# Fused attention and MLP block: the last head group of the last 256 queries in two passes, w_mod in three loads, and new settings for the order planner

## Chip, cores, metric

One core of one Trainium2 chip. The metric is device time of the core in microseconds (us). Engines are named as the profile has them: PE (TensorE products, with PEld for its weight loads), ACT (ScalarE), DVE (VectorE), POOL, SP (issues the transfers).

## The reference

One transformer block on 2048 tokens of 640 channels, bf16, 32 heads of 20, MLP width 1536. Cut to what matters:

```python
mod = (silu(c) @ w_mod).reshape(1, 6, 1, -1)            # sa, ca, ga, sb, cb, gb
h = layernorm(x) * (1 + ca) + sa
x = x + ga * attention(h, wqkv, wo)                     # 32 heads, softmax over 2048 keys
h = layernorm(x) * (1 + cb) + sb
x = x + gb * mlp(h, w1, b1, w2, b2)                     # layernorm, gelu (tanh form), inside
```

## The kernel before

The program lists every operation with an estimated duration, and a greedy planner in Python simulates the five engines and fixes, before the kernel is built, the order of each engine's instructions. At run time each engine goes through its list in order. An estimate is therefore never a time, but it decides the order.

The work is cut into head groups (4 heads) and query chunks. A tile is 512 columns of scores for one head: PE makes them, ACT takes the exp of two tiles at once, PE multiplies with V. DVE takes some tiles off ACT with a three-instruction polynomial. "Fillers" are products with zeros that only keep PE's clock up. The last 512 queries are two halves, HA (queries 1536 to 1791) and HB (1792 to 2047); their head groups 5 to 7 come last, HA's and then HB's.

```python
dma("sp", wm0[:, :, 0:D], wmod_v[:, :, 0:D], 819200)          # byte count: for the planner only
dma("sp", wm0[:, :, D:2 * D], wmod_v[:, :, D:2 * D], 819200)
...
for m in range(10):                                          # shift (0-4), scale (5-9) of the first layer norm
    for kt in range(KD):
        mm(bb[:, m:m + 1], wm0[:, kt, m * 128:(m + 1) * 128], s_col[:, kt:kt + 1], ..., name="mod")
...
# HA's section: partial sums of wo over head groups 0-4, for HA and HB
for i in range(8):
    add(h0 + P0 + P1 * i, 0.9 * P1, lambda pace, i=i: wo_job(HA + i // 4, ..., range(GS), None, "part"))
run_chunk(seq, aux, ...)
# HB's section
seq = [(HB, g) for g in range(GS, NG)]
...                                                          # HA: rest of wo, layer norm, transposes
run_chunk(seq, aux, lambda s: s < HS, 1e9)                   # DVE may take exps up to mark HS = 16 of 32
# after the last exp: PV, row sums, rest of wo, layer norm of both HB tiles, then
for ft in range(NL, KF): m1_act(HA, ft, 4, [acts[-1]])       # NL = 0; gelu, so behind the last exp's table
...
for i in range(4): ...                                       # m2 of HA
tr2(ci, [None] * 3, ["dve", "act", "dve"], prio=3)           # transposes of HB, 256 columns
for ft in range(KF): m1_act(ci, ft, 4)                       # m1 of HB
for i in range(2 * nt): ...                                  # m2 of HB
```

m1 is the first MLP product with its gelu, m2 the second; wo is the attention's output product.

The softmax here doesn't subtract the row's maximum and nothing guards it: scores larger than these inputs give would overflow.

## Time and profile before

| | before |
|---|---|
| median of 3 runs | 866.95 us (866.79 to 867.98) |
| span of the profiled run | 865.8 us, mean clock 0.996 |
| exp tiles on ACT / on DVE | 1695 / 353 |
| first score product | 19.91 us |
| end of the last exp | 829.67 us |
| from there to the end | 36.1 us |
| fillers on PE, 750 to 830 us | 10.5 us |

How to read it: the span falls into a start (until exps run without a gap), a long middle in which ACT is never free, and a tail after the last exp, in which ACT no longer matters.

### The profile page before, as it was taken

The page shows a single profiled execution, that of the slowest core. Times are in us where ns is not written, and L with a number is a line of the kernel's source. Part 1 is how long each engine was busy: PE and PEld are TensorE (multiplying, and loading weights), DVE is VectorE, ACT ScalarE, POOL GpSimd, SP SyncE. Part 2 cuts the span into 40 slices and gives each one's busy share as a digit, 9 for nine tenths or more (in the row PEclk, how much of TensorE's full clock was granted, in tenths as well). Part 3 has the DMA queues.
Part 4 walks back from the last instruction along what each step waited for, and adds up shares of the span by engine and source line. Part 5 has one row for each costly group of instructions (what it writes and reads, how often), then busy time and mean ns, then how long its engine had stood idle before and what let it go on. Part 6 is the DMA issues. An engine that isn't in the chain of part 4 may idle for free.

```text
span 865.8 us, 16443 instructions
## 1 busy us (share of the span) xinstructions
PE 851.4 (98%) x6626; PEld 294.3 (34%) x6626; DVE 790.2 (91%) x1587; ACT 824.9 (95%) x892; POOL 195.0 (23%) x462
## 2 busy tenths in 40 slices
PE   8999999999999999999999999999999999999998
PEld 3433333333332222323233333233333322333365
DVE  6948899999999999999999999999999999999571
ACT  3999999999999999999999999999999999999962
POOL 5500100026010000399102550000019200010020
PEclk8999999999999999999999999999999999999999
DMA  9500000011010001600000100101000000000000
GB/s 293 160 2 4 23 13 14 14 32 70 15 42 4 14 14 34 205 14 14 14 1 21 37 29 15 44 1 44 29 15 14 14 14 13 11 27 16 16 8 31
DMA packets 29071, 30.14 MB, mean 35 GB/s; under 512 B 11202, under 2 KB 23362, under 8 KB 28994
## 3 DMA queue, kind: packets, MB, share of 16 engines
q1 hardware_dynamic: 28994, 29.08, 10.6%
q8 instruction: 52, 0.85, 0.4%
q14 instruction: 25, 0.20, 0.1%
HBM read 26.07 MB, written 2.88 MB: 33 GB/s over the span
## 4 chain that ended last, share of the span: by engine, by line
PE 46%; DVE 28%; ACT 22%; DMA 3%; issue 0%; POOL 0%; SPq 0%; DVEq 0%
ACT arena L1040 20%; PE psum L749 19%; PE psum L1023 17%; DVE arena L1050 8%; DVE arena L1056 8%; PE psum L1087 8%; DVE arena L1053 5%; PE psum L835 3%; DMA arena<-in_B_w_dram 2%; DVE arena L1379 2%; ACT arena L1386 1%; DVE arena L945 1%; DMA arena<-in_w_mod_dram 1%; PE psum L755 1%; DVE arena L950 1%; DVE arena L1095 1%
## 5 line engine op out<-in xcount | busy, mean ns | idle before, releaser
L1040 ACT ACTIVATE arena<-psum 128x1024 bf16<-128x1024 f32 x846 | 781.3, 1103 | 4.8 <-PE psum L1023 3.4
L1023 PE MATMUL psum<-arena 32*128 32x512 bf16 (+1 forms) x2240 | 362.6, 365 | 4.6 <-ACT arena L1040 1.6
L749 PE MATMUL psum<-arena 128*128 128x320 bf16 (+6 forms) x1704 | 343.6, 308 | 4.6 <-DMA arena<-in_w_mod_dram 2.3
L1050 DVE TENSOR_SCALAR arena<-psum 128x512 f16<-128x512 uint16 x353 | 234.1, 679 | 17.7 <-PE psum L1023 16.2
L1056 DVE SCALAR_TENSOR_TENSOR arena<-psum,arena 128x512 uint16<-128x512 f32 x353 | 236.4, 680 | 2.6
L1023 PEld LDWEIGHTS psum<-arena 32*128 32x128 bf16 x2240 | 94.3, 91 | 274.0 <-ACT arena L1040 206.0
L1087 PE MATMUL psum<-arena 128*32 128x512 bf16 (+1 forms) x2240 | 182.4, 368 | 0.7 <-DVE arena L1095 0.7
L749 PEld LDWEIGHTS psum<-arena 128*128 128x128 bf16 (+1 forms) x1704 | 126.0, 97 | 156.9 <-issue 104.0
L1133 POOL TENSOR_TENSOR arena<-arena 128x128 bf16<-128x128 bf16 x124 | 52.9, 455 | 529.2 <-DMA arena<-scr 529.2
L1053 DVE TENSOR_TENSOR arena<-arena 128x512 f16<-128x512 f16 x353 | 147.8, 437 | 1.6
L835 PE MATMUL psum<-arena 128*128 128x512 bf16 (+3 forms) x278 | 83.8, 376 | 0.0
L1087 PEld LDWEIGHTS psum<-arena 128*32 128x32 bf16 x2240 | 43.4, 92 | 90.6 <-issue 79.8
L1358 POOL TENSOR_TENSOR arena<-arena 128x128 bf16<-128x128 bf16 x120 | 51.1, 455 | 9.9 <-DVE arena L903 9.9
L1301 POOL TENSOR_TENSOR arena<-arena 128x128 bf16<-128x128 bf16 x105 | 44.1, 454 | 19.7 <-DVE arena L1216 18.4
L891 DVE BATCH_NORM_STATS2 arena<-arena 128x6 f32<-128x320 bf16 x96 | 43.5, 477 | 0.4
L835 PEld LDWEIGHTS psum<-arena 128*128 128x128 bf16 x278 | 23.5, 99 | 39.5 <-issue 33.2
L1399 DVE TENSOR_TENSOR arena<-psum,arena 128x320 bf16<-128x320 f32 x32 | 15.5, 484 | 21.9 <-PE psum L749 21.8
L950 DVE TENSOR_SCALAR arena<-psum,arena 128x512 bf16<-128x512 f32 x31 | 23.0, 741 | 6.9 <-PE psum L749 6.9
L898 POOL TENSOR_SCALAR arena<-arena 128x1 f32<-128x1 f32 (+1 forms) x40 | 9.5, 239 | 84.0 <-DVE arena L893 84.0
L1379 DVE TENSOR_SCALAR arena<-psum,arena 128x512 bf16<-128x512 f32 x36 | 26.6, 739 | 0.0
L1095 DVE CAST arena<-psum 128x512 bf16<-128x512 f32 (+1 forms) x35 | 22.2, 635 | 3.6 <-PE psum L1087 3.6
L899 POOL TENSOR_TENSOR arena<-arena 128x1 f32<-128x1 f32 (+1 forms) x40 | 24.9, 624 | 1.8
(56 smaller groups left out, 213.1 us busy)
## 6 DMA issues: line engine op xcount, KB each, us to landing
arena<-scr SPq DMA_DIRECT2D x29, 256.0 KB
arena<-in_A_x_dram SPq DMA_DIRECT2D x6, 640.0 KB, 5.3
arena<-in_B_w_dram SPq DMA_DIRECT2D x2, 1920.0 KB
arena<-in_w_mod_dram SPq DMA_DIRECT2D x2, 1600.0 KB
out_dram<-arena SPq DMA_DIRECT2D x16, 160.0 KB, 1.8
arena<-in_A_wqkv_dram SPq DMA_DIRECT2D x3, 800.0 KB
arena<-in_w_mod_dram SPq DMA_DIRECT2D x2, 800.0 KB
arena<-in_A_x_dram SPq DMA_DIRECT2D x4, 320.0 KB
```

The lines of the kernel that those rows point to most:

```text
L749: return P.op("pe", lambda e: e.matmul(outp, lhsT, rhs, start=start, stop=stop), R=[lhsT, rhs], W=[outp], dur=d, lat=d + 0.17, prio=prio, ...
L835: return lambda e: e.matmul(d_, zero, r_, start=new, stop=new, skip_group_check=True)
L1023: r = e.matmul(o_, lh, rh, start=True, stop=True, tile_position=(32 * hl, 0))
L1040: return e.activation(ring3[:, s_[0]:s_[1] + 1:s_[1] - s_[0], :], src, ACTF.Exp, scale=ESC, bias=EBIAS)
L1050: d1 = P.op("dve", lambda e: e.tensor_scalar(vw_, m_, -65536.0 * QRHO, math.sqrt(QK2) / 65536.0, op0=ALU.add, op1=ALU.mult), dur=t_, lat=t ...
L1053: d2 = P.op("dve", lambda e: e.tensor_tensor(vw_, vw_, vw_, op=ALU.mult), dur=t2, lat=t2 + 0.095, prio=DP, name="d2", lock=True)
L1056: x.emit = lambda e: e.scalar_tensor_tensor(out=o_, in0=pb, scalar=QS0, in1=vw_, op0=ALU.add, op1=ALU.add)
L1087: r = e.matmul(o_, lh, rh, start=(kt == 0), stop=(kt == TT - 1), tile_position=(0, 32 * hl))
L1133: pool(lambda e, d1_=d1_, r1_=r1_: e.tensor_tensor(d1_, d1_, r1_, op=ALU.mult), [d1_], [d1_, r1_], dur=0.1 + 0.0021 * PSTEP, prio=3, name= ...
L1301: pool(lambda e, t_=t_, s_=s_, r_=r_: e.tensor_tensor(t_, s_, r_, op=ALU.mult), [t_], [s_, r_], dur=0.1 + 0.0021 * (b - a), prio=7)
L1358: pool(lambda e, op=op, t_=t_, r_=r_: e.tensor_tensor(t_, t_, r_, op=op), [t_], [t_, r_], dur=0.1 + 0.0021 * (b - a))
L1379: dve(lambda e: e.tensor_scalar(d, bb, b_, None, op0=ALU.add), [bb, b_], [d], n, dur=0.1 + n / 900., prio=2, name="m1ev")
```

## The change

Three intents. In the tail: do the last head group of HB in two passes of 128 queries (HT0, HT1), so that tile 0's wo and layer norm run beside tile 1's exps and the MLP goes tile by tile; three of HA's twelve m1 jobs move into filler room before the last exp; HA's wo is done in one go, without partial sums, and HB's partial sums move from HA's section into HB's. At the start: w_mod in three loads with a second accumulator, and byte counts that make the planner see transfers land later. And settings of the planner: `QLAT` (a latency margin in us), `FAR` (look-ahead), `BACK` (limit of DVE's backlog), `FILL` (threshold for fillers). Cut to its core:

```diff
-NL = 0
-P0, P1, ... = 4, 2, 3, 1, 9, .7, 16, 0
-OKT, RB = 3, 550000
-QLAT, TIGHT, PAIR = 0.6, 8, 2
-NEAR, FAR, BACK = 9, 20, 2.2
-FLOOR, FILL, WARM = 3400, 5400, 3072
+WS = 1024
+NL = 3
+P0, P1, ... = 7.5, 0.5, 3, 1, 9, .7, 16, 0
+OKT, RB = 3, 300000
+QLAT, TIGHT, PAIR = .7, 8, 2
+NEAR, FAR, BACK = 9, 19, 2.0
+FLOOR, FILL, WARM = 3400, 5000, 3072
...
-        dma("sp", wm0[:, :, 0:D], wmod_v[:, :, 0:D], 819200)
-        dma("sp", wm0[:, :, D:2 * D], wmod_v[:, :, D:2 * D], 819200)
+        dma("sp", wm0[:, :, 0:D], wmod_v[:, :, 0:D], 1350000)
+        for a, b in ((D, WS), (WS, 2 * D)):
+            dma("sp", wm0[:, :, a:b], wmod_v[:, :, a:b], 1280 * (b - a))
...
-                    for tl in reversed(range(nt)):
+                    for tl in (range(nt) if mod and not after else reversed(range(nt))):
...
-            wo_job(ci, i // 2, i % 2, pace, range(GS, NG), "part", None, 0)
+            wo_job(ci, i // 2, i % 2, pace, range(NG), None, None, 0)
...
-        for i in range(8):
-            add(h0 + P0 + P1 * i, ...)                      # partial sums in HA's section
...
-        seq = [(HB, g) for g in range(GS, NG)]
+        seq = [(HB, g) for g in range(GS, NG - 1)] + [(HT0, NG - 1), (HT1, NG - 1)]
+        for i in range(4):                                  # HB's partial sums, in HB's section
+            add(P0 + P1 * i, 0.3, lambda pace, i=i: wo_job(HB, ..., range(GS), None, "part"))
...
+            if c == HT1:                                    # tile 0: row sums, wo, layer norm beside the exps
+                add(u + 0.5, 0.3, lambda pace: sel_job(HT0, NG - 1, pace, 1))
+                for half in range(2):
+                    add(u + U1 + U2 * half, ...wo_job(HB, 0, half, pace, range(GS, NG), "part", None, 0, 1))
+                add(u + U1 + 1.5 * U2, 0.3, lambda pace: ln2(HB, 0, True))
...
         for tl in range(nt):                                # MLP per tile of 128
+            tr2(ci, [None], [TE], prio=3, only=tl)
+            for ft in range(KF):
+                m1_act(ci, ft, 4 if tl else M0, [acts[-1]], tl)
             for half in range(2):
+                m2_late(ci, tl, half, 5 if tl else M2)
```

(One weight copy also goes from ACT to DVE at the start, the row sums get a buffer of their own, and more banks serve the first projections.)

More of the change, by code (lines that the diff above doesn't have):

```diff
@@ L14 @@
 DP = 3.5
-NL = 0
-P0, P1, HW0, HW1, HT, HM, HS, WP = 4, 2, 3, 1, 9, .7, 16, 0
+U1, U2, M0, M2, TE = 1.5, 0.5, 4, 5, "dve"
+WS = 1024
+NL = 3
+P0, P1, HW0, HW1, HT, HM, HS, WP = 7.5, 0.5, 3, 1, 9, .7, 16, 0
 VP = 3
-OKT, RB = 3, 550000
+OKT, RB = 3, 300000
 TRE, VE = (["act", "dve", "act"], ["dve", "dve", "dve"]), ("dve", "dve")
@@ L625, in bass_adaLN_cond__mha_block__mixer_channel_mlp__prompt_kernel @@
     QK2, QRHO, QS0 = 43.16024758, 0.50767267, -10.90298758
-    QS = [(0, 512), (512, 512), (1024, 512), (1536, 512), (1536, 256), (1792, 256)]
+    QS = [(0, 512), (512, 512), (1024, 512), (1536, 512), (1536, 256), (1792, 256), (1792, 128), (1920, 128)]
     LAST, HA, HB, GS = 3, 4, 5, 5
-    SLOT = (0, 1, 0, 1, 1, 1)
-    COL = (0, 0, 0, 0, 0, 256)
+    HT0, HT1 = 6, 7
+    SLOT = (0, 1, 0, 1, 1, 1, 1, 1)
+    COL = (0, 0, 0, 0, 0, 256, 256, 384)
     es = ExitStack()
@@ L718, in bass_adaLN_cond__mha_block__mixer_channel_mlp__prompt_kernel @@
         modc = V(alloc(64), [16], F32)
+        modc2 = V(alloc(64), [16], F32)
         b1col = V(alloc(64), [KF], F32)
@@ L794, in bass_adaLN_cond__mha_block__mixer_channel_mlp__prompt_kernel @@
         dma("sp", c_row[0:KD, :], c[0].rearrange("(kt p) -> kt p", p=128), 1280)
-        dma("sp", xb[0][:, 0:2, :], xsrc(0, 256), 327680)
-        dma("sp", xb[0][:, 2:4, :], xsrc(256, 256), 327680)
-        dma("sp", wm0[:, :, 0:D], wmod_v[:, :, 0:D], 819200)
-        dma("sp", wm0[:, :, D:2 * D], wmod_v[:, :, D:2 * D], 819200)
+        dma("sp", xb[0][:, 0:2, :], xsrc(0, 256), 560000)
+        dma("sp", xb[0][:, 2:4, :], xsrc(256, 256), 400000)
+        dma("sp", wm0[:, :, 0:D], wmod_v[:, :, 0:D], 1350000)
+        for a, b in ((D, WS), (WS, 2 * D)):
+            dma("sp", wm0[:, :, a:b], wmod_v[:, :, a:b], 1280 * (b - a))
         for w in (1, 0):
@@ L860, in bass_adaLN_cond__mha_block__mixer_channel_mlp__prompt_kernel @@
         dve(lambda e: e.tensor_copy(s_col, c_col), [c_col], [s_col], KD, prio=0)
-        bb = aux_bank()
+        bb, bb_ = aux_bank(), aux_bank()
+        WM = WS // 128
         for m in range(10):
             for kt in range(KD):
-                mm(bb[:, m:m + 1], wm0[:, kt, m * 128:(m + 1) * 128], s_col[:, kt:kt + 1],
+                mm((bb if m < WM else bb_)[:, m:m + 1], wm0[:, kt, m * 128:(m + 1) * 128], s_col[:, kt:kt + 1],
                    kt == 0, kt == KD - 1, 0, 1, cyc=130, name="mod")
         dve(lambda e, bb=bb: e.tensor_copy(modc[:, 0:5], bb[:, 0:5]), [bb[:, 0:5]], [modc[:, 0:5]], 5, prio=0)
-        dve(lambda e, bb=bb: e.tensor_scalar_add(modc[:, 5:10], bb[:, 5:10], 1.0), [bb[:, 5:10]], [modc[:, 5:10]],
-            5, prio=0)
+        for b_, m0, m1 in ((bb, 5, WM), (bb_, WM, 10)):
+            dve(lambda e, b_=b_, m0=m0, m1=m1: e.tensor_scalar_add((modc if m0 == 5 else modc2)[:, m0:m1], b_[:, m0:m1], 1.0), [b_[:, m0:m1]],
+                [(modc if m0 == 5 else modc2)[:, m0:m1]], 5, prio=0)
         for w in (1, 0):
@@ L876, in bass_adaLN_cond__mha_block__mixer_channel_mlp__prompt_kernel @@
                     pool(lambda e, dst=dst, src=src: e.tensor_copy(dst, src), [dst], [src], dur=0.5, prio=2)
+                elif w:
+                    act(dst, src, ACTF.Copy, n=400, prio=1)
                 else:
-                    act(dst, src, ACTF.Copy, n=400, prio=1)
+                    dve(lambda e, dst=dst, src=src: e.tensor_copy(dst, src), [src], [dst], 400, prio=2)
         for w in (1, 0):
@@ L907, in tr_jobs @@
         def tr_jobs(hn_tile, nt, dst, mod, prio, rels, engs, after=()):
-            for i, ktp in enumerate(((0, 1), (2, 3), (4,))):
+            for i, ktp in enumerate(((0, 1), (2, 3), (4,)) if nt > 1 else (tuple(range(KD)),)):
                 tb = aux_bank().bitcast(BF16)
                 for j, kt in enumerate(ktp):
-                    for tl in reversed(range(nt)):
+                    for tl in (range(nt) if mod and not after else reversed(range(nt))):
                         tr(tb[:, (j * nt + tl) * 128:(j * nt + tl + 1) * 128],
@@ L927, in tr_jobs @@
                     d = dst(kt, 1)
-                    s1, s2 = modc[:, 5 + kt:6 + kt], modc[:, kt:kt + 1]
+                    s1, s2 = (modc if 5 + kt < WM else modc2)[:, 5 + kt:6 + kt], modc[:, kt:kt + 1]
                     if engs[i] == "act":
@@ L1095, in pv_row @@
                 dve(lambda e: e.tensor_copy(d_, acc), [acc], [d_], n, prio=0, name="pvcopy")
+        rinv2 = V(o_kT + 3 * S * 2, [512], F32)
         def sel_job(ci, g, pace=NOPACE, prio=6, step=None):
@@ L1104, in sel_job @@
             for a in range(0, n, step):
-                s_, r_, d_ = bb[:, a:a + step], rinv[:, a:a + step], d[:, a:a + step]
+                s_, r_, d_ = bb[:, a:a + step], rinv2[:, COL[ci] + a:COL[ci] + a + step], d[:, a:a + step]
                 dve(lambda e, s_=s_, r_=r_: e.reciprocal(r_, s_), [s_], [r_], step, dur=0.07 + 3.2 * step / 512,
@@ L1162, in bass_adaLN_cond__mha_block__mixer_channel_mlp__prompt_kernel @@
                      dur=0.22, lat=0.4, prio=2, mode="f", name="warm", wc=512)
-                set_banks([5, 7])
+            set_banks([5, 7] if tc else [5, 7, 2, 3])
             for g in range(2):
@@ L1167, in bass_adaLN_cond__mha_block__mixer_channel_mlp__prompt_kernel @@
                     proj_job(g, 0, tc, g)
+            set_banks([5, 7])
             for tl in range(4):
@@ L1334, in wo_evac, with wo_job @@
             dve(lambda e: e.tensor_tensor(d, bb, s_, op=ALU.add), [bb, s_], [d], 320, prio=prio, name="x2")
-        def wo_job(ci, tl, half, pace, gs=range(NG), src=None, dst=None, prio=2):
+        def wo_job(ci, tl, half, pace, gs=range(NG), src=None, dst=None, prio=2, pp=6):
             bb = aux_bank()[:, 0:320]
-            mmjob(bb, wo_pairs(ci, tl, half, gs), 320, 6, pace, "wo")
+            mmjob(bb, wo_pairs(ci, tl, half, gs), 320, pp, pace, "wo")
             wo_evac(ci, tl, half, bb, prio, src, dst)
@@ L1362, in ln2, with tr2 @@
             normalize(hd, hd, tt, p, so=4)
-        def tr2(ci, rels, engs, prio=6):
+        def tr2(ci, rels, engs, prio=6, only=None):
             h2T = views(ci)[2]
+            if only is not None:
+                tr_jobs(lambda tl: hn_of(ci, only), 1, lambda kt, n: h2T[:, kt:kt + n, only * 128:(only + 1) * 128], False,
+                        prio, rels, engs)
+                return
             tr_jobs(lambda tl: hn_of(ci, tl), QS[ci][1] // 128, lambda kt, n: h2T[:, kt:kt + n, :], False,
@@ L1456, in bass_adaLN_cond__mha_block__mixer_channel_mlp__prompt_kernel @@
             add(h0 - 8, 0.1, lambda pace, x=x: load_x2(x))
-        for i in range(8):
-            add(h0 + P0 + P1 * i, 0.9 * P1, lambda pace, i=i: wo_job(HA + i // 4, i % 4 // 2, i % 2, pace, range(GS), None, "part"))
         run_chunk(seq, aux, lambda s: s >= TWO, TWO, (7, 4))
         aux.clear()
-        seq = [(HB, g) for g in range(GS, NG)]
+        seq = [(HB, g) for g in range(GS, NG - 1)] + [(HT0, NG - 1), (HT1, NG - 1)]
         add(0.5, 0.3, lambda pace: sel_job(HA, NG - 1, pace, 1, step=128))
@@ L1465, in bass_adaLN_cond__mha_block__mixer_channel_mlp__prompt_kernel @@
             add(HW0 + HW1 * i, 0.6, wo_late(HA, i))
+        for i in range(4):
+            add(P0 + P1 * i, 0.3, lambda pace, i=i: wo_job(HB, i // 2, i % 2, pace, range(GS), None, "part"))
         add(HT, 0.3, lambda pace: tr2(HA, pace.rels(3), ["dve"] * 3))
@@ L1470, in bass_adaLN_cond__mha_block__mixer_channel_mlp__prompt_kernel @@
         for j, (c, g) in enumerate(seq):
-            if j:
+            if c == HT1:
+                add(u + 0.5, 0.3, lambda pace: sel_job(HT0, NG - 1, pace, 1))
+                for half in range(2):
+                    add(u + U1 + U2 * half, 0.3, lambda pace, half=half: wo_job(HB, 0, half, pace, range(GS, NG), "part", None, 0, 1))
+                add(u + U1 + 1.5 * U2, 0.3, lambda pace: ln2(HB, 0, True))
+            elif c == HT0:
+                add(u + 0.5, 0.3, lambda pace: sel_job(HB, NG - 2, pace, 1, step=128))
+            elif j:
                 add(u + 2, 0.3, lambda pace, x=seq[j - 1]: sum_job(*x))
@@ L1482, in bass_adaLN_cond__mha_block__mixer_channel_mlp__prompt_kernel @@
             gelu(HA, NOPACE, after=[acts[-1]], loads=1.4, k=NL)
-        early = [(tl, half) for tl in range(nt) for half in range(2)]
+        early = [(1, half) for half in range(2)]
         wbank = {}
@@ L1489, in bass_adaLN_cond__mha_block__mixer_channel_mlp__prompt_kernel, with m1_act @@
         set_banks([7, 4, 5, 6])
-        sel_job(ci, NG - 1, prio=1, step=128)
-        def m1_act(ci, ft, prio, after=()):
-            n = QS[ci][1]
+        sel_job(HT1, NG - 1, prio=1)
+        def m1_act(ci, ft, prio, after=(), tl=None):
+            c0, n = (0, QS[ci][1]) if tl is None else (tl * 128, 128)
             bb = aux_bank()[:, 0:n]
             for i, (l, r) in enumerate(m1_pairs(ci, ft)):
-                mm(bb, l, r, i == 0, i == KD - 1, prio, n, name="m1")
+                mm(bb, l, r[:, c0:c0 + n], i == 0, i == KD - 1, prio, n, name="m1", rel=len(marks) - 1)
@@ L1497, in m1_act, with m2_late @@
             b_ = b1col[:, ft:ft + 1]
-            d_ = g1_of(ci)[:, ft, :]
+            d_ = g1_of(ci)[:, ft, c0:c0 + n]
             P.op("act", lambda e: e.activation(d_, bb, ACTF.Gelu_apprx_tanh, bias=b_), R=[bb, b_], W=[d_],
                  dur=n / 1200.0 + 0.235, lat=n / 1200.0 + 0.435, prio=2, name="gelu1", after=after)
+        def m2_late(ci, tl, half, prio=5):
+            bb = aux_bank()[:, 0:320]
+            for ft, (l, r) in enumerate(m2_pairs(ci, tl, half)):
+                mm(bb, l, r, ft == 0, ft == KF, prio, 320, name="m2")
+            finish_y(ci, tl, half, bb)
@@ L1502, in bass_adaLN_cond__mha_block__mixer_channel_mlp__prompt_kernel @@
         for ft in range(NL, KF):
             m1_act(HA, ft, 4, [acts[-1]])
+        for tl, half in early:
+            bb = wbank[(tl, half)]
+            (l, r), = wo_pairs(ci, tl, half, [NG - 1])
+            mm(bb, l, r, False, True, 3, 320, name="wo")
+            wo_evac(ci, tl, half, bb, 0, "part")
+        ln2(ci, 1, tail=True)
+        for i in range(4):
+            m2_late(HA, i // 2, i % 2)
+        set_banks(range(8))
         for tl in range(nt):
+            tr2(ci, [None], [TE], prio=3, only=tl)
+            for ft in range(KF):
+                m1_act(ci, ft, 4 if tl else M0, [acts[-1]], tl)
@@ L1505, in bass_adaLN_cond__mha_block__mixer_channel_mlp__prompt_kernel @@
             for half in range(2):
-                bb = wbank[(tl, half)]
-                (l, r), = wo_pairs(ci, tl, half, [NG - 1])
-                mm(bb, l, r, False, True, 3, 320, name="wo")
-                wo_evac(ci, tl, half, bb, 0, "part")
-            ln2(ci, tl, tail=True)
-        for i in range(4):
-            bb = aux_bank()[:, 0:320]
-            for ft, (l, r) in enumerate(m2_pairs(HA, i // 2, i % 2)):
-                mm(bb, l, r, ft == 0, ft == KF, 5, 320, name="m2")
-            finish_y(HA, i // 2, i % 2, bb)
@@ L1516, in bass_adaLN_cond__mha_block__mixer_channel_mlp__prompt_kernel @@
-        set_banks(range(8))
-        tr2(ci, [None] * 3, ["dve", "act", "dve"], prio=3)
-        for ft in range(KF):
-            m1_act(ci, ft, 4)
-        for i in range(2 * nt):
-            bb = aux_bank()[:, 0:320]
-            for ft, (l, r) in enumerate(m2_pairs(ci, i // 2, i % 2)):
-                mm(bb, l, r, ft == 0, ft == KF, 5, 320, name="m2")
-            finish_y(ci, i // 2, i % 2, bb)
+                m2_late(ci, tl, half, 5 if tl else M2)
         P.final = outs
```

## The prediction

> **What bounds the kernel now.** I read the busy table first, then the page in 40 slices, then narrow stretches at both ends, then the time-ordered chain and the time-ordered instructions of the tail.
>
> ```profile
> PE 851.4 (98%) x6626; PEld 294.3 (34%) x6626; DVE 790.2 (91%) x1587; ACT 824.9 (95%) x892; POOL 195.0 (23%) x462
> ACT  3999999999999999999999999999999999999962
> PEclk8999999999999999999999999999999999999999
> ...
> L1040 ACT ACTIVATE arena<-psum 128x1024 bf16<-128x1024 f32 x846 | 781.3, 1103 | 4.8 <-PE psum L1023 3.4
> L835 PE MATMUL psum<-arena 128*128 128x512 bf16 (+3 forms) x278 | 83.8, 376 | 0.0
> ```
>
> PE shows 98%, but 83.8 us of it are fillers (L835, they only keep the clock up). The engine without slack is ACT: its exps (L1040) fill all slices but the first and the last two. 781.3 us / 846 = 0.92 us for a pair of score tiles, 0.46 us for one 512-column tile. So three things decide the time: when the exps start, how many tiles DVE takes off ACT, and what is left after the last exp. The busy table by stretch (columns: length, then PE, PEld, DVE, ACT, POOL, granted clock, DMA share, GB/s):
>
> ```profile
> 12.00:18.00 6.00, 6.00 (x45) 3.67 (x43) 3.89 (x12) 3.49 (x6) 2.87 (x6) 0.50 1.00 337
> 24.00:30.00 6.00, 6.00 (x54) 2.56 (x52) 6.00 (x16) 6.00 (x8) 5.54 (x12) 1.00 0.20 44
> 791.00:808.00 17.00, 16.99 (x213) 6.66 (x208) 14.75 (x31) 17.00 (x20) 0.00 (x0) 1.00 0.02 2
> 808.00:820.00 12.00, 11.97 (x138) 4.50 (x136) 4.81 (x12) 12.00 (x15) 1.60 (x4) 1.00 0.08 26
> 832.30:847.30 15.00, 15.00 (x117) 11.01 (x118) 12.00 (x31) 5.68 (x12) 3.50 (x8) 1.00 0.04 13
> 848.50:863.00 14.50, 14.49 (x112) 10.54 (x112) 1.47 (x3) 5.71 (x13) 0.00 (x0) 1.00 0.07 24
> ```
>
> At the start PE runs at a clock of 0.50 while it is 100% busy. At the end PE is busy 29.5 of 29.5 us while ACT is at 38% and DVE idles in the second half. The chain of work that ended last says the same at both ends (start, length, what):
>
> ```profile
> 11.58 0.83 PE psum L749 x25
> 12.41 2.16 PE psum L755 x20
> ...
> 15.84 3.07 PE psum L749 x9
> 18.93 0.75 DVE arena L945
> ...
> 832.29 15.07 PE psum L749 x116
> ...
> 848.46 14.54 PE psum L749 x112
> 863.00 0.02 issue
> 863.02 0.49 DVE arena L1399
> ```
>
> **What the Trainium skill says.**
> 1. "TensorE: Matmul & The Clock Gate", Part 1: the array falls to half clock after an idle window of about 3.4 us and comes back after a busy one[...]. The trace agrees: PE idles from 7.6 to 9.4 and most of 11.0 to 11.6 (0.63, 0.00, 0.57 busy in the single microseconds 7 to 10), the products with w_mod are one column wide, and the clock is 0.50 from 11.4 to 17.9.
> 2. Same page, "Back-to-back issue gap": a sustained stream of weight load and 128-column product is put at about 81 ns. The trace disagrees: ten 128-wide transposes with a weight load each issue in 0.56 us, 56 ns apiece, and 25 one-column products with new weights take 0.76 us, 30 ns apiece. I use 56 ns.
> 3. "ScalarE: Activation LUTs", "What ACT_TABLE_LOAD costs": a table load is 1283 ns (the trace has 1.28 us before the gelu), and an activation with a pointer bias takes 280 ns + 0.833 ns per column, neighbours overlapping by 93 ns. For 128 columns that makes an estimate of 0.29 us; no such shape is in the trace.
>
> **The change part by part.**
>
> *Start.* The three loads of w_mod move the same bytes. The byte counts given to the scheduler become larger, so that its simulated landing is later; it should then put transposes and fillers where PE now waits (7.6 to 9.4, 11.0 to 11.6). Transposes go in tile order and the first three scale columns have their own accumulator, so evacuations can begin before the last w_mod part lands (11.57 now). One 0.53 us weight copy moves from ACT, where it sat between two evacuations of hT (14.06), to DVE. On the chain, PE work from 11.58 to 18.93 is 7.3 us, of which 6.5 at half clock. At full clock: mod products done at 12.35, 20 transposes 1.1 us (now 2.16) to 13.5, with the first evacuation at about 12.9; three ACT evacuations of 0.72 end at about 15.0; last K product and five Q products (0.22 each) to 16.3; Q evacuation 0.75; first scores at 17.1 where they are now at 19.9. **Start: -2.8 us.** It carries to the end, since ACT has no idle time from 23.1 on, as long as DVE (100% from 20 to 30) still prepares the next 512 tokens in time; that work moves forward too.
>
> *Exps.* 2048 tiles remain; a pass of 128 queries packs four key tiles in a 512-column tile, so ACT's work is the same. The 32 tiles of the last group need 8 score products of 128 columns where 4 of 256 stood: by 56 ns against 107 ns nothing to speak of, and 25 fillers (4.5 us) stood in the last 10 us of exps, so PE has room. But DVE gets other work. A tile on DVE costs about 1.46 us net of overlap (in 700 to 720: 20 us less 4.6 of other work, 10.5 tiles). Only the first 48 of the last 96 tiles may go to DVE; it now does 8 there (791 to 808), with some 3.5 us of other work and 2.25 idle. The old kernel's wo and second layer norm of the first 128-query tiles ran late (812 to 827), because a backlog of partial wo products on PE came first. The new one drops that partial sum for HA (8 products in one go), so these land on time, in the very stretch where DVE should take exps. Each layer norm is 4.1 us of DVE (2 x 0.49 + 0.21 stats twice, 0.40 norm twice, 2 x 0.50): I put about 5 us more there, 3 to 4 tiles fewer on DVE, 3.5 x 0.46 = 1.6 us more on ACT. Against it, three evacuations of 0.48 leave the stretch before (one tile more on DVE, -0.46). In the last 48 tiles DVE had 12 of 21.7 us to do; the new sum (sel of the sixth group 2.3, of the first pass 1.2, two wo 1.0, layer norm 4.1, three m1 evacuations 1.3) is about 10, and fits. The small knobs (look-ahead, DVE backlog, filler threshold) I take as nothing. **End of the exps: +1.0 us.**
>
> *Tail.* After the last exp (829.7) PE is the bound: 33.3 us to the last product. Leaving it, into PE's filler room before: 15 of 60 m1 products of HA (6.45 us / 60 = 107 ns each) 1.6 us; HA's ten transposes, 0.7; half of the early and final wo products, 4 x 0.156 + 2 x 0.14 = 0.9. Together 3.2. Coming in: m1 of the last 256 queries as 120 products of 56 instead of 60 of 107, +0.3; one small wait at the second tile's transposes, +0.1. The m2 sums (13 products, 1.975 each, eight of them) stay. **Tail: -2.8 us.**
>
> Sum: -2.8 + 1.0 - 2.8 = -4.6, on 866.95: 862.3 us.
>
> **Rivals.**
> - *The tail's chain through the last tile becomes the bound.* For tile 1: PV and its copy 1.7 us, row sums and reciprocal 1.9, wo 1.3, layer norm with POOL hops 6.4, transposes 1.2, m1 with twelve gelus 4, m2 4.0, all after 829.7: 20.5 us. PE has 30 us to do, and 20 us of it (nine m1, HA's m2, tile 0's MLP) need nothing from tile 1. So it should hide; if the order put m2 of HA too early or too late, PE would stand for 1 to 3 us: 864 to 865.
> - *The half tile is issue-bound.* At 81 ns for 128 columns the 120 products take 9.7 us, not 6.7: 3 us, and the tail gains nothing: 865.
> - *The start is held by transfers.* DMA is saturated from 3 to 24 us (share 1.0). w_mod's last part can't land before 11.57, and x comes after it. If the early clock is won but ACT then waits for hT of the second 512 tokens, the start keeps only 1 us: 864. For it: DVE is full from 20 to 30. Against it: ACT has 32 tiles, 14.7 us of work, from the first tokens.
> - *The knobs were retuned well.* If DVE takes 5 more tiles over the 700 us in the middle, that is another -2.3: 860. The trace (DVE 97% busy there) leaves little.
>
> **Range and chances.** The three terms have errors of about 1.5, 1.5 and 1.5 us, and the knobs 1: some 2.8 together, so 8 in 10 lie within about 3.6 on either side; I widen it a little on the fast side, since a change with so many settings was most likely tuned. 857.8 to 866.0. Two per cent is 17 us, more than half of the whole tail, and no path to it exists: within 2% 0.97, faster 0.02, slower 0.01.
>
> **What would show it.** Granted clock at 1.0 between 12 and 18 us and the first score product near 17 (start right; at 0.5 it is wrong). ACT dense from about 20.5. The last exp near 828 (829.7 - 2.8 + 1.0). DVE exps among the last 96 tiles down from 8 to about 5. From the last exp to the end 33.3 us where it is 36.1, PE without a gap over 0.5 us, 128-column m1 products at 56 ns. PE gaps in the tail, products at 80 ns, or an ACT gap between 25 and 40 us would each prove one term wrong.

## More of the kernel before

The stretches around the last exp, in the table of busy time by stretch (columns: length, then PE, PEld, DVE, ACT, POOL, clock, DMA share, GB/s):

```profile
790.00:829.67 39.67, 39.56 (x469) 15.63 (x469) 27.39 (x62) 39.66 (x44) 5.27 (x12) 1.00 0.04 12
829.67:832.29 2.62, 2.04 (x26) 1.19 (x25) 1.34 (x5) 1.28 (x1) 0.00 (x0) 1.00 0.03 6
832.29:863.00 30.71, 30.25 (x238) 22.15 (x238) 14.50 (x37) 11.96 (x25) 3.50 (x8) 1.00 0.05 17
```

PE is full before and behind the last exp, and only before it does it hold fillers.

## The result, and the profile after

861.57 us (859.86 to 862.16, 4 runs) against 867.19 in the same rounds: ratio 0.9931, 95% interval 0.9914 to 0.9948. A ratio is the mean time of one kernel's fast runs over that of the other's of the same rounds, so not quite the ratio of the medians. At a bar of 2% that counts as the same, to which the prediction gave 0.97. The predicted time was 862.3 in a range of 857.8 to 866.0. The total is right. The terms are not: this table compares the two profiled runs.

| | before | after | predicted for after |
|---|---|---|---|
| mean clock | 0.996 | 0.998 | (no cold window) |
| first score product | 19.91 | 20.26 | 17.1 |
| end of the last exp | 829.67 | 827.44 | 827.9 (-2.8 + 1.0) |
| exp tiles on DVE | 353 | 356 | fewer in the last 96, otherwise the same |
| last exp to the end | 36.1 | 33.0 | 33.3 |
| span | 865.8 | 860.4 | 861.2 |

The page of the changed kernel, lines as shown of before:

```profile
PE 836.7 (97%) x6710; PEld 296.0 (34%) x6768; DVE 797.5 (93%) x1601; ACT 821.5 (95%) x898; POOL 194.7 (23%) x460
L1049 ACT ACTIVATE arena<-psum 128x1024 bf16<-128x1024 f32 x845 | 779.4, 1105 | 4.4 <-PE psum L1032 3.8
L840 PE MATMUL psum<-arena 128*128 128x512 bf16 (+3 forms) x230 | 74.1, 394 | 0.0
```

Fillers fell by 9.7 us (83.8 to 74.1). Of the exp work on ACT, 2.7 us went (with the single tiles: 781.3 + 2.2 to 779.4 + 1.4), which is more than the 2.2 us by which the last exp came earlier. So the start gave nothing in this run. By 60 us its ACT had 37.9 us of exps done, that of the kernel before 38.8: it was even 0.9 us behind (one_pass, nl0 and hs24 below, with the same start and the same mean clock, had 38.5 to 38.8, so part of this is the single run). Its stretches say why:

```profile
9.00:10.00 1.00, 0.28 (x4) 0.11 (x3) 0.04 (x1) 0.00 (x0) 1.00 (x3) 1.00 1.09 321
11.00:12.00 1.00, 0.39 (x16) 0.30 (x13) 0.97 (x2) 0.00 (x0) 0.46 (x1) 1.00 0.67 171
12.00:13.00 1.00, 0.58 (x21) 0.44 (x19) 0.61 (x3) 0.00 (x0) 0.76 (x2) 1.00 0.79 168
13.00:14.00 1.00, 1.00 (x21) 0.88 (x19) 0.26 (x2) 0.59 (x2) 0.58 (x3) 0.97 0.92 326
16.00:17.00 1.00, 1.00 (x4) 0.38 (x3) 1.00 (x4) 0.00 (x0) 0.00 (x0) 0.50 1.04 371
```

PE still waits for w_mod and the clock is halved again, in one window (13.9 to 17.4) and no longer in two (11.1 to 18.0; the prediction reads 11.4 to 17.9). The last part of w_mod lands at 12.7, not at 11.6; DMA is only 0.67 to 0.79 busy while it comes. The tail, in the same table by stretch:

```profile
790.00:827.44 37.44, 37.34 (x571) 17.71 (x569) 29.85 (x69) 37.44 (x41) 4.22 (x12) 1.00 0.03 7
827.44:829.64 2.20, 1.28 (x25) 0.65 (x23) 0.65 (x2) 1.81 (x3) 0.45 (x1) 1.00 0.03 7
829.64:857.60 27.96, 27.76 (x275) 20.60 (x275) 12.71 (x31) 10.99 (x33) 2.42 (x6) 1.00 0.06 19
```

PE's part behind the table load fell from 30.71 to 27.96 us, without gaps. In the stretch before it PE idles 0.92 of 2.20 us; that wait is new and was not foreseen. The chain of waits names it (start, length, what):

```profile
826.39 1.36 PE psum L753 x9
...
827.81 1.28 ACT L1522
829.10 0.01 issue
829.11 0.48 ACT arena L1522
829.59 0.05 issue
829.64 0.24 PE psum L753
```

HA's m1 products are ready early, fill the four banks open to them, and PE then waits until ACT has loaded its gelu table (1.28 us) and emptied one. The same chain then runs through DVE, from 829.90 to 835.49 (last row sums, both layer norms), and PE waits 0.16 us for it at 835.5: up to there PE and DVE are all but tied. Fillers between 750 and 830 us fell from 10.5 to 3.3 us: the room that the moved work went into is nearly used up.

### The profile page after: what moved, and what is told of

The parts are those of the page before. It is cut to its first block, busy times and chain, and to the rows that moved or that the text cites. A ratio compares the mean times of both kernels' runs of the same rounds, so it can differ in the third digit from the quotient of the medians.

```text
span 860.4 us, 16684 instructions
## 1 busy us (share of the span) xinstructions
PE 836.7 (97%) x6710; PEld 296.0 (34%) x6768; DVE 797.5 (93%) x1601; ACT 821.5 (95%) x898; POOL 194.7 (23%) x460
## 4 chain that ended last, share of the span: by engine, by line
PE 48%; ACT 37%; DVE 12%; DMA 1%; issue 1%; SPq 0%; ACTq 0%
ACT arena L1049 35%; PE psum L753 18%; PE psum L1032 18%; PE psum L1096 9%; DVE arena L1059 3%; DVE arena L1065 3%; PE psum L840 3%; DVE arena L1062 2%; ACT arena L1402 1%; DMA arena<-in_w_mod_dram 1%; PE psum L759 1%; DVE arena L900 1%; DVE arena L959 1%; DVE arena L977 1%; DVE arena L1395 0%
## 5 line engine op out<-in xcount | busy, mean ns | idle before, releaser
L1049 ACT ACTIVATE arena<-psum 128x1024 bf16<-128x1024 f32 x845 | 779.4, 1105 | 4.4 <-PE psum L1032 3.8
L1032 PE MATMUL psum<-arena 32*128 32x512 bf16 (+2 forms) x2304 | 367.6, 359 | 9.3 <-DVE arena L1065 2.7
L753 PE MATMUL psum<-arena 128*128 128x320 bf16 (+6 forms) x1708 | 328.3, 300 | 8.3 <-issue 3.9
L1059 DVE TENSOR_SCALAR arena<-psum 128x512 f16<-128x512 uint16 x356 | 236.2, 680 | 14.4 <-PE psum L1032 12.7
L1032 PEld LDWEIGHTS psum<-arena 32*128 32x128 bf16 x2304 | 98.7, 91 | 266.8 <-ACT arena L1049 188.0
L1096 PE MATMUL psum<-arena 128*32 128x512 bf16 (+5 forms) x2304 | 181.7, 362 | 1.2 <-DVE arena L1104 0.7
L1096 PEld LDWEIGHTS psum<-arena 128*32 128x32 bf16 (+1 forms) x2304 | 44.3, 93 | 90.4 <-issue 78.7
L840 PE MATMUL psum<-arena 128*128 128x512 bf16 (+3 forms) x230 | 74.1, 394 | 0.0
L1395 DVE TENSOR_SCALAR arena<-psum,arena 128x512 bf16<-128x512 f32 (+1 forms) x39 | 28.1, 720 | 0.1
L959 DVE TENSOR_SCALAR arena<-psum,arena 128x512 bf16<-128x512 f32 x31 | 23.0, 742 | 4.7 <-PE psum L753 4.7
L912 DVE TENSOR_SCALAR arena<-arena 128x640 bf16<-128x640 bf16 x48 | 23.2, 497 | 3.0 <-POOL arena L908 3.0
L1104 DVE CAST arena<-psum 128x512 bf16<-128x512 f32 (+2 forms) x36 | 22.3, 621 | 3.3 <-PE psum L1096 3.3
```

The costliest lines, as they stand in the source:

```text
L753: return P.op("pe", lambda e: e.matmul(outp, lhsT, rhs, start=start, stop=stop), R=[lhsT, rhs], W=[outp], dur=d, lat=d + 0.17, prio=prio, ...
L840: return lambda e: e.matmul(d_, zero, r_, start=new, stop=new, skip_group_check=True)
L1032: r = e.matmul(o_, lh, rh, start=True, stop=True, tile_position=(32 * hl, 0))
L1049: return e.activation(ring3[:, s_[0]:s_[1] + 1:s_[1] - s_[0], :], src, ACTF.Exp, scale=ESC, bias=EBIAS)
L1059: d1 = P.op("dve", lambda e: e.tensor_scalar(vw_, m_, -65536.0 * QRHO, math.sqrt(QK2) / 65536.0, op0=ALU.add, op1=ALU.mult), dur=t_, lat=t ...
L1096: r = e.matmul(o_, lh, rh, start=(kt == 0), stop=(kt == TT - 1), tile_position=(0, 32 * hl))
```

## The experiments

Each kernel was timed in 5 rounds (null_dp in 6) beside the kernel before, but not beside the changed kernel; the median of the kernel before was 866.89 to 867.19 in the four sets of rounds. Instruction lists were compared too: in some variants they differ only around the edited place, in others the planner reorders thousands of lines in the middle. That decides what a variant can tell. Because runs differ in the cold window at the start, the means at a mean clock of 0.998 and of 1.0 stand beside the median. The changed kernel has only three runs at 0.998 (861.05 to 862.16) and one at 1.0, so a difference of less than about 1 us to it isn't clear of noise. "Exp end" and "tail" are of the profiled run.

| kernel | lists differ | median | ratio to before (95%) | mean at 0.998 / 1.0 | exp end | tail |
|---|---|---|---|---|---|---|
| changed kernel | | 861.57 | 0.9931 (0.9914 to 0.9948) | 861.77 / 859.86 | 827.44 | 33.0 |
| start_only | from before: start | 866.62 | 0.9990 (0.9976 to 1.0004) | 866.87 / 865.53 | 828.57 | 36.1 |
| start_undone | widely | 863.82 | 0.9962 (0.9950 to 0.9975) | 864.14 / none | 827.25 | 35.2 |
| one_pass | last section | 862.80 | 0.9955 (0.9943 to 0.9968) | 862.72 / none | 826.77 | 34.2 |
| old_knobs | widely | 863.91 | 0.9966 (0.9953 to 0.9978) | 863.74 / none | 829.31 | 33.1 |
| warm_start | start | 862.12 | 0.9943 (0.9931 to 0.9954) | 862.89 / 861.32 | 828.20 | 32.9 |
| two_loads | start | 860.49 | 0.9926 (0.9914 to 0.9939) | 861.63 / 860.13 | 826.77 | 32.9 |
| null_qlat | widely | 862.97 | 0.9953 (0.9941 to 0.9965) | 863.47 / 861.91 | 829.63 | 32.1 |
| null_dp | widely | 868.75 | 1.0016 (1.0004 to 1.0029) | 869.02 / 867.32 | 829.89 | 34.9 |
| warm_fill | from two_loads: 8 products | 861.27 | 0.9934 (0.9922 to 0.9947) | none / 861.29 | 826.64 | 33.0 |
| nl0 | tail | 862.66 | 0.9947 (0.9934 to 0.9959) | 862.53 / 860.85 | 827.08 | 33.8 |
| old_partials | last sections | 864.42 | 0.9975 (0.9961 to 0.9988) | 865.56 / 863.99 | 825.12 | 37.0 |
| hs24 | last section | 863.58 | 0.9959 (0.9947 to 0.9972) | 863.75 / 862.36 | 824.72 | 37.0 |

One run of null_dp (899.36 us at a clock of 0.96) is left out of its ratio. "Exp end" contains the luck of the start: the profiled runs of start_only, null_dp, warm_fill and old_partials had a clock of 1.0, that of start_undone 0.996, all others 0.998. All outputs were correct.

**start_only: the kernel before with the change's start.**

```diff
+        dma("sp", wm0[:, :, 0:D], wmod_v[:, :, 0:D], 1350000)
+        for a, b in ((D, WS), (WS, 2 * D)): dma(...)        # and the other edits of the start
```

> The kernel before with the change's start alone (three loads of w_mod, larger byte counts for the scheduler, transposes in tile order, second scale tile, one weight copy moved to DVE). Theory from the two traces: the start gained nothing, since in the changed kernel the first score product came at 20.26 us against 19.91 and the clock was still halved from 14.0 to 17.2: 866 to 868.5 us, same as before, unless a run escapes the cold window (then about 865.5). Rival, the prediction on record: the start is worth 2.8 us: about 864.4.

The ratio 0.999 is 0.9 us of gain, with an interval of 2.1 gained to 0.3 lost: a gain of 2.8 is out. The profiled run had a clock of 1.0, its first score product was at 18.28, and by 60 us ACT had 40.6 us of exps done where the kernel before had 38.8. So a warm start can win 1.9 us by then, but the last exp ended only 1.1 us earlier, and three of the five runs were not fully warm. At a mean clock of 0.998 its two runs (866.87) equal the three of the kernel before in the same rounds (866.90), so what the start gains it gains in warm runs.

**start_undone: the changed kernel with the old start.**

```diff
-        dma("sp", wm0[:, :, 0:D], wmod_v[:, :, 0:D], 1350000)
+        dma("sp", wm0[:, :, 0:D], wmod_v[:, :, 0:D], 819200)   # and the other edits of the start
```

> The changed kernel with the start of the kernel before. Theory: the start is worth nothing, so all of the gain stays: 861 to 862.5 us. Rival (prediction on record): the start carries half of the gain, so 864.4 us.

It lost 2.3 us in the median, near the rival's number, but not where the rival says: its last exp ended at 827.25, no later than with the new start. Its tail is 2.2 us longer. The planner had reordered the whole list, and in that order most of HA's early m1 work slid behind the last exp (PE has 59 products of 256 columns there, the changed kernel 46). So this run doesn't measure the start; start_only does.

**two_loads and warm_start: what in the start matters.**

```diff
 two_loads
-        for a, b in ((D, WS), (WS, 2 * D)):
+        for a, b in ((D, 2 * D),):
 warm_start
-        dma("sp", wm0[:, :, 0:D], wmod_v[:, :, 0:D], 1350000)
+        dma("sp", wm0[:, :, 0:D], wmod_v[:, :, 0:D], 1700000)
-                   ..., cyc=130, name="mod")
+                   ..., cyc=70, name="mod")
```

> The changed kernel with w_mod in two loads as before; the two scale tiles and all else stay. Order of instructions differs only near the start. Theory: the third load gives nothing: its last part landed at 12.7 us (11.6 before) with DMA only 0.67 to 0.79 busy[...]; with two loads the last part lands about 0.5 us earlier and the time is the same or 0.5 us less: 861.0 to 861.6. Rival: the earlier first evacuations are what the third load buys, and without it the start loses 1 us: 862.6.

> The changed kernel, with the scheduler told that the first part of w_mod lands 1 us later and that a one-column product takes 32 ns (70 columns) and not 57, so that it puts fillers into the waits between the three parts of w_mod. Instruction order differs from the changed kernel's only in the first 50 us. Theory: the clock still halves in the changed kernel because PE is only 0.28 to 0.68 busy from 9 to 13 us; filled, the clock stays at 1.0 and ACT's exps start 1.5 to 2.5 us earlier: 859.5 to 860.5. Rival: the start is held by the last w_mod landing and by DVE (full from 20 to 30 us), so a warm clock is worth less than 0.7 us: 861 to 861.6.

With two loads the time is the same at either clock (861.63 against 861.77 at 0.998, 860.13 against 859.86 at 1.0). The third load buys nothing measurable. warm_start went against my theory: three of five runs were warm, yet it is no faster, since at a clock of 0.998 it is 1.1 us slower (862.89).

**warm_fill: two loads, and zero products where PE waits for w_mod.** It differs from two_loads by eight products and nothing else.

```diff
+  before the mod products of m = 0, 5, 8: 4, 3 and 1 of
+      e.matmul(psum[:, 3072:3584], zero, idr, start=False, stop=False, skip_group_check=True)
```

> The kernel with two loads of w_mod, all orders unchanged, with eight zero products of 512 columns put in where PE waits for w_mod (4, 3 and 1 of them). In the changed kernel and its variants, runs at a mean clock of 1.0 (no cold window at the start) are 1.5 to 1.9 us faster than runs at 0.998. Theory: with the waits filled every run has a clock of 1.0 and the median is that of the two-load kernel's warm runs, 860.1 (859.8 to 860.4), with no run above 861. Rival: the fillers push w_mod's products back or the window is cold anyway: 860.5 to 861.5, some runs at 0.998.

All five runs had a clock of 1.0, as the theory said, and lay within 0.6 us (861.05 to 861.63). From 9.60 to 13.01 us, the 3.41 us before the clock fell in two_loads, PE was busy 3.39 us here and 2.57 there. Five warm runs of five beside three of five is little by itself; but in the kernels with the changed kernel's own start (changed kernel, nl0, one_pass, old_partials, hs24) 6 of 24 runs were warm. That idle PE brings on the cold window is thus likely, not proven. The rival was right on the time: it is 1.2 us slower than the warm runs of two_loads. In the two profiles the last products with w_mod start at 13.16 where two_loads had them done by about 13.0; the first score product is at 18.72 against 19.78 with a cold clock, and ACT had 39.5 against 38.4 us of exps done by 60 us. But the last exp ended at 826.64 against 826.77: nearly all of that lead was gone by then.

**one_pass: the last group in one pass of 256, the old MLP order behind it; the rest of the change stays.**

```diff
-        seq = [(HB, g) for g in range(GS, NG - 1)] + [(HT0, NG - 1), (HT1, NG - 1)]
+        seq = [(HB, g) for g in range(GS, NG)]              # and the tail of the kernel before
```

> The changed kernel with the last head group of the last 256 queries in one pass of 256 and the old tail after it; the three early m1 products, the moved partial sums, the start and the knobs are kept. Theory: the split lets tile 0's wo, layer norm and row sums run beside the last exps, so it is worth about 1 us of PE (wo and sel) and removes the wait for tile 0's layer norm: 862.5 to 863.5. Rival: the tail's gain of 3.5 us is the split's nearly alone: about 865. Second rival: the split costs as much in 128-column products as it saves: 861.5.

Its tail is 34.2 us, 1.2 longer, and at a clock of 0.998 it is 0.95 us slower (862.72 against 861.77). The split itself is worth about 1 us of the tail's 3.2. As totals the intervals of the two ratios overlap, so the size rests on the trace and on equal clocks, and of the changed kernel's three runs at 0.998 one (862.16) comes within 0.3 us of one_pass's fastest (862.43).

**nl0 and old_partials: the work moved ahead of the last exp.**

```diff
 nl0
-NL = 3
+NL = 0
 old_partials
+        for i in range(8): add(h0 + 4 + 2 * i, ...)         # HA and HB partials in HA's section, as before
-        for i in range(4): add(P0 + P1 * i, ...)            # HB partials in HB's section
-            wo_job(ci, i // 2, i % 2, pace, range(NG), None, None, 0)
+            wo_job(ci, i // 2, i % 2, pace, range(GS, NG), "part", None, 0)
```

> The changed kernel with none of HA's m1 jobs before the last exp (NL 0 instead of 3). Only the last 50 us of the lists differ. Prediction on record: 15 products leave the tail, 1.6 us: 863.2. Rival: with NL 0 the products come back at 107 ns each, but the 0.9 us gap of PE at the table load (it waits for a free bank) and three DVE evacuations go, so the loss is only 0.5 to 1 us: 862.1 to 862.6.

> The changed kernel with the partial wo sums of both halves (HA, HB) back in HA's section, as before. Theory: the backlog on PE returns, HA's second layer norm comes after the 48th tile, HA's transposes and the three m1 jobs slip past the last exp, while DVE may do one or two exps more before it: 862.5 to 864. Rival (prediction on record taken alone): DVE then has about 5 us less before the 48th tile and the exps end 1 us earlier, and the time is the same or better: 860.5 to 861.6.

nl0: tail 33.8 (+0.8), 862.53 against 861.77 at 0.998 (+0.8). Fifteen products of 107 ns are 1.6 us. The rival's number came, its reason did not: the wait for a bank is there with `NL` = 0 too, 0.86 us at 829.27.

```profile
829.27 6.58 PE L753 MATMUL psum<-arena 128*128 128x256 bf16 x57 [0.86 <-ACT arena L1522]
```

Behind the last exp nl0 has 58 products of 256 columns, the changed kernel 46: 12 more and not 15, since three got ahead of it anyway. PE is busy 1.1 us longer there (30.17 against 29.04) and stands 0.2 us less.

old_partials is the most telling of all: it ran 3.8 us longer at a clock of 0.998 (865.56 in two runs, against 861.77), with a tail of 37.0 us. Its exps ended at 825.12, 2.3 us before the changed kernel's, but that is the start: its profiled run was warm, and by 60 us ACT was 2.5 us ahead. The table by stretch, exps on ACT alone, the changed kernel first:

```profile
0.00:60.00 60.00, 37.87 (x41) 0.97 0.53 164
0.00:60.00 60.00, 40.38 (x44) 1.00 0.53 164
```

ACT's instructions around the last exp, in order of time (start, length, what, idle before):

```profile
825.14 1.28 ACT L1522 ACT_TABLE_LOAD   x1
829.93 0.47 ACT L1522 ACTIVATE arena<-psum,arena 128x256 bf16<-128x256 f32 x1 [3.51 <-PE psum L753]
840.24 0.83 ACT L1402 ACTIVATE arena<-arena 128x768 bf16<-128x768 bf16 x1
```

ACT waits 3.5 us for HA's first m1 product, and the gelu of the three early m1 jobs comes at 840.24; in the changed kernel the first gelu follows the table load at once and that of the three jobs is at 832.24. HA's layer norm had come too late: DVE stands from 802.9 to 808.7 waiting for PE, which has an m2 and the last two partial sums still to do (evacuated at 808.66, 810.64 and 813.23), and HA's transposes, done before 820 in the changed kernel, start at 827.26. Behind the last exp PE runs 3.0 us of fillers, where the changed kernel has none. (DVE took no more exps than in the changed kernel: 356, and 5 where that took 6 in 790 to 808.)

**hs24: DVE may take exps of the first 72 of the last 96 tiles.**

```diff
-P0, P1, ... HM, HS, WP = 7.5, 0.5, ... .7, 16, 0
+P0, P1, ... HM, HS, WP = 7.5, 0.5, ... .7, 24, 0
```

> The changed kernel with DVE allowed to take exps in the first 72 of the last 96 tiles, not 48. Theory: DVE is only 5 to 8 of 10 us busy from 800 to 828 while ACT is full, so it takes 3 to 5 tiles more, worth 0.46 us each: 859.5 to 860.5. Rival: the exps on DVE hold up tile 0's wo evacuations and layer norm, which then slip into the tail: 861.5 to 863.

DVE did take 3 more tiles and the exps ended 2.7 us earlier, at 824.72 (0.9 us of that it was ahead by 60 us, at the same mean clock). The tail grew by 4.0 us and the kernel is 2.0 us slower at a clock of 0.998. The rival was right:

```profile
824.75 1.28 ACT L1522 ACT_TABLE_LOAD   x1
834.28 0.84 ACT L1402 ACTIVATE arena<-arena 128x768 bf16<-128x768 bf16 x1 [3.05 <-DVE arena L1395]
```

The gelu of HA's three early jobs now waits 3.05 us for DVE, which still had their evacuations to do, and PE runs 3.1 us of fillers behind the last exp. Here, then, an earlier last exp went with a slower kernel; in old_partials the early end was the warm start's.

**old_knobs, and the two controls null_qlat and null_dp.**

```diff
 old_knobs
-QLAT ... = .7    FAR, BACK = 19, 2.0    FILL = 5000
+QLAT ... = 0.6   FAR, BACK = 20, 2.2    FILL = 5400
 null_qlat
-QLAT, TIGHT, PAIR = .7, 8, 2
+QLAT, TIGHT, PAIR = .69, 8, 2
 null_dp                                    (the planner's duration of a reciprocal of 16 columns)
-dur=0.2, prio=3, name="recip"
+dur=0.21, prio=3, name="recip"
```

> The changed kernel with the old look-ahead (20), DVE backlog limit (2.2), filler threshold (5400) and latency margin (0.6). Theory from the traces: by 750 us the changed kernel had some 6 more tiles done, about 2 us, and its ACT idled 1.2 us less between 60 and 790, so the knobs are worth 1.5 to 2.5 us: 863 to 864. Rival (prediction on record): the knobs are worth nothing: 861.6.

> Control. The changed kernel with the scheduler's latency margin at 0.69 instead of 0.70 us, a difference that means nothing to the chip but reorders some 4,400 lines of PE's list. Theory: two equal plans differ by 1 us or more by chance, so this loses 0.5 to 2.5 us against the changed kernel (862 to 864), and the 2 us that the old knobs lost are such a reordering. Rival: a margin of 0.7 is itself what helps, then 0.69 gives 861 to 862.

> Second control. The changed kernel with the scheduler's duration of one small reciprocal at 0.21 us instead of 0.20; all settings of the change stay, some 4,300 lines of PE's list move. Theory (chance of the plan): 862 to 864, as for the first control. Rival (the settings themselves help): 861 to 862.

The old settings cost 2.0 us at equal clock, nearly all of it before the last exp (829.31 against 827.44, with tails of 33.1 and 33.0). Building the lists again, which needs no chip, showed that `FAR` and `BACK` do not move a single instruction. `FILL` alone changes 7 lines of PE's list; beside the old `QLAT` it moves some 2000. So the loss comes from the new order that the latency margin `QLAT` brings, alone or together with `FILL`; no run separates the two. But 0.69 costs 1.7 us as well, and a change of 0.01 us in one planned duration costs 7.2 us, more than the whole change gained. Both controls keep all settings that mean something. The middle of null_dp and of the changed kernel, ACT being the fourth number after the length:

```profile
100.00:400.00 300.00, 298.48 (x2179) 93.77 (x2179) 294.41 (x565) 297.99 (x324) 75.90 (x180) 1.00 0.11 35
400.00:750.00 350.00, 346.62 (x2442) 110.07 (x2445) 340.45 (x674) 347.37 (x363) 83.03 (x198) 1.00 0.06 20
```

```profile
100.00:400.00 300.00, 292.81 (x2174) 94.17 (x2206) 295.22 (x569) 299.79 (x327) 73.14 (x174) 1.00 0.11 35
400.00:750.00 350.00, 343.49 (x2436) 110.54 (x2450) 340.97 (x673) 348.92 (x363) 85.31 (x204) 1.00 0.06 20
```

In 650 us ACT idles 4.6 us where the changed kernel's idles 1.3, almost all of it waiting for PE's scores, though DVE takes two tiles more (358). The tail is 1.9 us longer too. I expected 862 to 864 for this control; the chance in a plan is larger than I thought.

No variant beats the changed kernel clear of noise; two_loads (ratio 0.9926) is its equal with less code.

## Why the prediction was right or wrong

**Total: right** (862.3 predicted, 861.57 measured), by two errors that cancelled.

**Start, -2.8: mis-sized.** start_only measures -0.9 (-2.1 to +0.3). Two steps failed. First, "it should then put transposes and fillers where PE now waits": it did so only in part (PE 0.28, 0.39 and 0.58 busy at 9, 11 and 12 us), likely because the planner's landing times were still early and because it holds a one-column product for 57 ns where 25 of them take 0.78 us, 31 ns each; warm_start, which corrects both, still had two cold runs of five. Whether a window then comes out cold differs from run to run: one of four runs of the changed kernel was warm. Over all kernels here that have runs at both 0.998 and 1.0, the warm runs are 1.3 to 1.9 us faster. Second, even with a warm clock, first scores came at 18.0 to 18.7 and not 17.1, as the last products with w_mod began at 12.39 in start_only, where my sum starts them at 11.58. Even where they began at 11.84 (old_partials) the first scores came at 17.98, since PE's order puts other work between. And the lead of 1 to 2 us shrank again in a fixed order planned for other times (warm_fill). What eats it in the middle is not settled.

**Exps, +1.0: wrong in sign**, -2.2 measured at the last exp, with a start that was 0.9 us behind. The reasoning on the last 96 tiles held in part: DVE took 6 and not 8 in 790 to 808. That the moved partial sums are the reason is not shown: with the old ones (old_partials) it took 5. What failed is the step "The small knobs (look-ahead, DVE backlog, filler threshold) I take as nothing". The latency margin, which I had not even listed, reorders the middle; three more tiles landed on DVE (3 x 0.46 = 1.4 us of the 2.7 us of exp work that left ACT; the rest is single tiles and a slightly shorter pair) and ACT idled 1.3 instead of 2.0 us between 60 us and the last exp (0.7). With the old settings the last exp came 1.9 us later. The controls show that this is the luck of one plan among many near-equal ones, not a property of the value 0.7. My rival "the knobs were retuned well" came nearest.

**Tail, -2.8: right**, -3.2 measured (36.1 to 33.0), composed otherwise than I summed it. HA's m1 products gave 0.8 and not 1.6 (nl0): only 12 of the 15 left the tail, and PE stands 0.2 us more. The 0.9 us wait for a bank at the table load was not foreseen either, but it is there without them too. The split gave about 1 (one_pass). The moved partial sums, of which I only saw that they take DVE time before the 48th tile, are worth the most: without them 3.8 us are lost, because HA's transposes and early m1 then slip behind the last exp. The three losses (0.8, 1 and 3.8) add up to more than 3.2, since each was measured with the other two parts in place. 128-column m1 products take 60 ns (7.3 us for 121), so the rival of 81 ns falls. A gelu of 128 columns took 0.37 us where the prediction estimated 0.29; ACT had room for it. The rival that tile 1's chain becomes the bound falls too: from 829.64 PE idles 0.2 of 28 us.

**A step taken for granted that the runs correct:** that an earlier last exp is an earlier end. hs24 ends its exps 2.7 us earlier (1.8 after taking off the lead of its start) and finishes 2.0 later. Near the end PE is the bound on both sides of the last exp; what counts is how much of its work sits in front, where fillers stood, and so whether DVE has that work's inputs ready in time.

## What to carry to other kernels

Near the end, count the filler or idle time of the engine that bounds the tail, and ask what can be moved into it; the moment at which another engine finishes is worth nothing by itself. Where a planner fixes the order, test a change against controls that mean nothing (0.01 us in one estimate): here they move the time by 1.7 and 7.2 us, so a difference of a few us between two plans is evidence for a mechanism only if the lists stay the same elsewhere. Sort runs by the mean clock before comparing them: a run without a cold window was 1.3 to 1.9 us faster, as much as most parts of this change. That is not a constant: in the kernel before, one cold window instead of two was worth 0.5 us (7 runs, mean 866.64, against 22, mean 867.13). Compare the work done by a fixed early time, too, before reading a later moment of two profiles: old_partials would have been misread without it.

## What the Trainium skill lacked or had wrong

- "TensorE: Matmul & The Clock Gate", "Back-to-back issue gap": about 81 ns for a sustained stream of weight load and 128-column product. Here 56 ns (transposes) and 60 ns (m1, mixed with 320-column products).
- Same page, Part 1: it says that the window is free-running and that the same kernel can start cold or warm. The runs agree: one unchanged list ran at a mean clock of 0.998 and of 1.0. The page gives no measure of how much a short product counts as activity (of transposes it says, in Part 4, that they don't count as busy in the same way). In two_loads PE was busy 2.57 of the 3.41 us before the clock fell at 13.0, 1.55 of them in 50 one-column products; in start_only it was busy 2.49 of 3.41 us from 10.86 on, 0.93 of them in 25 such products, and the clock stayed at 1.0. So the busy share alone doesn't tell. Eight more 512-column zero products kept the clock at 1.0 in five of five runs.
- "DMA: Bandwidth & Descriptors", "Why small descriptors are slow (HBM only)", works out a penalty for descriptors of 256 bytes, and the page's specifications give 512 bytes as the least for line rate. Here DMA was 0.67 to 0.79 busy while the third part of w_mod, in rows of just 512 bytes, came in (11 to 13 us); in two_loads, without such rows, it was 1.00 to 1.05 busy then. Issuing three loads took SP 2.36 us where two took 1.04. Whether the rows or the issue slowed it was not separated.
- No page warns that a static order is itself a source of spread: 0.01 us in one planned duration cost 7.2 us.
